# Attention and spectral filter in one kernel: arithmetic of the combination and of the maxima moved to GpSimd, the reciprocal's gate to ScalarE, and a transposition moved one step later

## Chip, cores and metric

One core of one Trainium2 chip. The metric is the device time of one execution in microseconds, as a median over runs; a profiled execution of the same kernel gives the trace, whose span runs from the first to the last instruction.

## What is computed

Two independent parts, joined along the last axis. Part A is an attention with a compressive memory: 2048 rows of width 576, 32 heads of width 18, four segments of 512 rows. In each segment s and head:

```python
logits = qs @ ks.T * scale + causal_mask
a_dot  = softmax(logits) @ vs
pq     = phi(qs)                       # t+1 for t>0, else exp(t)
a_mem  = (pq @ M) / (pq @ z + 1e-6)    # memory of the segments before
o      = g * a_mem + (1 - g) * a_dot   # g = sigmoid(beta), one per head
M, z   = M + phi(ks).T @ vs, z + sum(phi(ks))
```

The heads are joined again and multiplied by wo. Part B is a two-dimensional real FFT of another 2048 x 576 input, a product with a complex filter, and the inverse FFT. All is float32; most matrix products split their inputs into a high and a low part, so that a value x becomes a rounded copy h and a remainder l = x - h, each of which goes through TensorE.

## The kernel before

The order of all instructions on every engine is that in which the Python code issues them; nothing reorders it. Generators that yield let several strands of work be interleaved by hand. The stages are: the forward FFT (to about 78 us), the projections of part A interleaved with the middle of part B (to about 285 us), the inverse FFT with the first ten score blocks of the attention (to about 376 us), and the attention loop with its end (to 818 us). The change lies in the last two.

**The attention loop** (`ATT.attention`, L809 to L877) runs 133 steps t. Four steps, hh = t % 4 = 0 to 3, make one group k = t // 4 of four heads; two groups are one n, eight groups (32 steps) one segment g.

- `s1` (L595 to L616), ten steps ahead: the scores of one head with queries on the partitions, in four matrix products (L602), each followed on VectorE by one reduction with the mask (L606), which puts the row maxima of 128 queries into a column of the tile `mg`. A step has reductions over 128, 384, 512 and 256 elements.
- `mpath` (L617 to L632), once for each group: TensorE transposes the 16 columns of `mg` (L621) into one of the three PSUM buffers that `s1` uses; ScalarE copies the result out as `mf` (L626) and rounds it to bfloat16, `mts[:,0]` (L627); a DMA on GpSimd's queue (L623) writes that as row 108 of the query tile `Qs`; VectorE computes the remainder `mts[:,1]` (L630), and a second DMA writes row 109. These two rows stand against rows of -1 in `Ks` and so subtract the maximum from the scores. The group that is k + 2 in this step starts its `mpath` at hh = 2 and ends it at hh = 3 (L854 to L858). In the prologue (L794 to L808) the first two groups do the same.
- `s2` (L633 to L658): the scores again with keys on the partitions and with the two added rows (L641 to L650), exponentials on ScalarE into P (L642, L647, L651), and after each group four masking operations on GpSimd (L653), 128 x 512 each.
- `pv` (L659 to L670): P times the values (L668), five steps after the exponentials of its group began. `pv_out` copies the result U (L674), and DMAs on SP write it and the sums of the softmax to DRAM (`u_dmas`).

**Background work.** `run_bg(1.2)` (L820 to L826) advances the first generator of the list `bg` 1.2 times in each step; a list `lane` is advanced once in each step, ahead of it. For each segment:

- `recip` (L686 to L706), in `lane`: load the sums as `rx` (SP), three yields, add 1e-6 where asked (L693), reciprocal (L695), multiplication by the gate (L696), rounded copy (L698) and remainder (L699), all on VectorE; store on SP, two yields, load as `rr` or `rd`. It runs seven times: at step 41, 71 and 103 for the memory, at step 45, 77 and 109 and after the loop for the softmax.
- `combine` (L749 to L773), in `bg`: three loads `ux` on SP, two yields, then seven passes t. Pass t spreads the reciprocals over the rows of each head (L765, TensorE into the single PSUM buffer "post"), multiplies `ux` by it (L770, or L768 in segment 0) and adds the memory's part `am` (L771, not in segment 0), both on VectorE. Two passes later the sum is rounded by ScalarE (`oh`, L760) and VectorE computes the remainder (`ol`, L761). Passes 0 and 1 load the fourth and fifth `ux` into buffers that the first two have left.
- `mem1` (L732 to L744): the memory's part of the next segment, with one multiplication on VectorE (L742).
- `oproj` (L774 to L790): the product with wo, 15 matrix products (L786) for each of eight blocks, copied out by ScalarE (L788) from the single "post" buffer, and stored on SP (L789).

After step 132 the rest of `bg` and the last `recip` are advanced in turns (L871 to L875), and then `combine(3)` and `oproj(3)` run alone.

## Time and profile before

| | |
|---|---|
| median of three runs | 826.8 us (824.0 to 826.88) |
| the profiled execution | 820.21 us, span 818.2 us |
| mean granted TensorE clock | 0.96 |
| TensorE, matrix products busy | 727.3 us (89%) |
| VectorE busy | 611.9 us (75%) |
| ScalarE busy | 472.3 us (58%) |
| GpSimd busy | 181.0 us (22%) |

The profiled execution lies 6.6 us under the median of the three runs. Lines of the profile name the line of the kernel, the engine, the operation, the tiles (out<-in) and their shape; in the grouped rows "| busy us, mean ns | idle time before, and what ended it |" follows, in rows in order of time the first two numbers are the start and the duration in us. PE is TensorE, PEld its weight loads, DVE VectorE, ACT ScalarE, POOL GpSimd, SP the queue that issues most DMAs.

### The profile page before, as it was taken

What the parts mean: (1) busy time and instruction counts of PE and PEld (TensorE: products, weight loads), DVE (VectorE), ACT (ScalarE), POOL (GpSimd) and SP (SyncE); (2) the same over time, 40 slices, a digit from 0 to 9 for tenths busy, and PEclk for the clock granted to TensorE, in tenths of its full rate; (3) what the DMA queues carried; (4) which work ended last, traced back from release to release, by engine and by line L of the source; (5) the groups of instructions that cost most, each with busy time, mean ns of one, the idle gap of its engine ahead of it and who ended that gap; (6) DMA issues with size and microseconds to landing.
All of it is one profiled execution on the core that took longest, in us unless ns stands there. A gap on an engine that the chain in (4) does not pass through costs nothing.

```text
span 818.2 us, 14656 instructions
## 1 busy us (share of the span) xinstructions
PE 727.3 (89%) x4751; PEld 489.2 (60%) x4751; DVE 611.9 (75%) x1687; ACT 472.3 (58%) x996; POOL 181.0 (22%) x340
## 2 busy tenths in 40 slices
PE   5998999999999969997988988899988999978856
PEld 4887788797897958895333333335542345523645
DVE  5999877895878779986788888886778767792040
ACT  2665894846846534444777755666555665657111
POOL 2110001001001164441553331331312231323000
PEclk9999999999999989999999989999996999989969
DMA  8883434653534778735576556564463644310221
GB/s 305 264 253 116 158 139 152 223 176 119 196 120 168 255 160 204 223 124 143 146 182 144 123 125 163 132 153 122 115 167 92 156 120 120 115 37 17 61 86 58
DMA packets 82496, 121.27 MB, mean 148 GB/s; under 512 B 9368, under 2 KB 49430, under 8 KB 82284
## 3 DMA queue, kind: packets, MB, share of 16 engines
q1 hardware_dynamic: 74836, 104.29, 44.2%
q0 software_dynamic: 7584, 16.05, 6.7%
q8 instruction: 38, 0.62, 0.3%
q14 instruction: 38, 0.31, 0.1%
HBM read 81.75 MB, written 38.35 MB: 147 GB/s over the span
## 4 chain that ended last, share of the span: by engine, by line
PE 60%; DVE 21%; ACT 8%; issue 6%; DMA 3%; SPq 1%; POOL 0%; DVEq 0%; ACTq 0%
PE pj L440 10%; PE po L786 8%; DVE junk L606 8%; PE s L602 8%; PE pv L668 7%; PE pjv L440 7%; PE i L292 3%; PE i L303 3%; PE s L641 2%; PE s L645 2%; PE pn L735 2%; PE pm L497 1%; DMA Qs<-qkD 1%; PE s L650 1%; DVE eo L123 1%
## 5 line engine op out<-in xcount | busy, mean ns | idle before, releaser
L606 DVE CUSTOM_DVE_ANT_0 junk<-s,mask 128x128 bf16<-128x128 f32 (+3 forms) x512 | 251.3, 491 | 71.6 <-PE s L602 27.1
L602 PE MATMUL s<-Ks,Qs 108*128 108x128 bf16 (+3 forms) x512 | 138.2, 313 | 19.5 <-DVE mg L606 16.2
L602 PEld LDWEIGHTS <-Qs 108*128 108x128 bf16 x512 | 47.1, 100 | 114.4 <-issue 100.9
L668 PE MATMUL pv<-P,vs 128*32 128x512 f32 (+3 forms) x1024 | 100.0, 463 | 1.0 <-issue 0.8
L642 ACT ACTIVATE P<-s 128x512 f32<-128x512 f32 x128 | 76.8, 600 | 41.5 <-PE s L641 34.7
L623 POOL DMA_DIRECT2D Qs<-mts x64 | 31.7, 496 | 247.3 <-ACT mts L627 184.3
L651 ACT ACTIVATE P<-s 128x256 f32<-128x256 f32 x128 | 49.1, 383 | 64.2 <-PE s L650 60.1
L647 ACT ACTIVATE P<-s 128x512 f32<-128x512 f32 x128 | 76.3, 596 | 7.5 <-PE s L646 5.6
L653 POOL TENSOR_SCALAR_AFFINE_SELECT P<-P 128x512 f32<-128x512 f32 x128 | 77.0, 641 | 14.2 <-ACT P L642 13.8
L440 PE MATMUL pj<-xh,wqkh 128*128 128x512 f32 x180 | 71.2, 395 | 0.5 <-ACT Z L151 0.5
L440 PE MATMUL pj<-xh,wqkl 128*128 128x512 f32 x180 | 71.1, 395 | 0.0
L440 PE MATMUL pj<-xl,wqkh 128*128 128x512 f32 x144 | 61.8, 429 | 0.0
L641 PE MATMUL s<-Qs,Ks 110*128 110x512 bf16 x128 | 51.2, 400 | 3.6 <-ACT P L642 2.8
L202 DVE TENSOR_TENSOR Z<-t,t 128x290 f32<-128x290 f32 (+1 forms) x96 | 53.0, 598 | 0.2
L292 PE MATMUL i<-civ,Y 128*128 128x256 f32 (+1 forms) x288 | 44.4, 308 | 9.4 <-DVE T L320 5.3
L202 DVE TENSOR_TENSOR t<-Z 128x580 f32<-128x580 f32 x64 | 48.0, 788 | 0.2
L440 PE MATMUL pjv<-wvh,xh 128*128 128x288 f32 x160 | 48.1, 303 | 0.0
L292 PEld LDWEIGHTS i<-civ,Y 128*128 128x128 f32 (+1 forms) x288 | 39.8, 199 | 11.7 <-DVE T L320 6.3
L440 PE MATMUL pjv<-wvl,xh 128*128 128x288 f32 x160 | 46.2, 295 | 0.0
L645 PE MATMUL s<-Qs,Ks 110*128 110x384 bf16 x128 | 43.5, 340 | 0.1
L606 DVE DVE_READ_ACCUMULATOR2_ANT mg<- 128x1 f32 x512 | 42.4, 83 | 0.1
L788 ACT COPY ob<-po 128x288 f32<-128x288 f32 x32 | 12.7, 398 | 48.3 <-PE po L786 48.1
(140 smaller groups left out, 1518.7 us busy)
## 6 DMA issues: line engine op xcount, KB each, us to landing
qkD<-sp SPq DMA_DIRECT2D x36, 384.0 KB
Qs<-qkD SPq DMA_DIRECT2D x96, 144.0 KB
Ks<-qkD SPq DMA_DIRECT2D x96, 144.0 KB
xin<-xb SPq DMA_DIRECT2D x16, 384.0 KB
cfw<-cfw POOLq DMA_DIRECT2D x16, 384.0 KB, 4.4
civ<-civ POOLq DMA_DIRECT2D x16, 384.0 KB, 7.1
vs<-vD SPq DMA_DIRECT2D x16, 330.0 KB
vD<-vt SPq DMA_DIRECT2D x16, 311.0 KB
```

Of the source, the lines that this page charges most:

```text
L202: v.tensor_tensor(o,a,b,op=op)
L292: nc.tensor.matmul(p[:m,k],Y[i][:,q,c*128:c*128+m],cc[:,hl,o:o+256],start=n==0,stop=n==5)
L440: s.nc.tensor.matmul(out,a,b,start=i==0,stop=i==len(L)-1)
L602: nc.tensor.matmul(out,Q[:108,h,128*i:128*i+128],K[:108,h,:128*(i+1)],start=True,stop=True)
L606: nc.vector.tensor_tensor_reduce(out=junk[:,:w],in0=src,in1=s.mask[:,512-w:],scale=1.0,scalar=-3.0e38, op0=OP.add,op1=OP.max,accum_out=s.m ...
L641: nc.tensor.matmul(p0,kk(0),q(0),start=True,stop=True)
L642: nc.scalar.activation(P[0][:,hh],p0,AF.Exp,scale=SC)
L645: nc.tensor.matmul(p1[:,:384],kk(1),q(128),start=True,stop=True)
L647: nc.scalar.activation(P[1][:,hh],p1,AF.Exp,scale=SC)
L653: sel=lambda x,pat: nc.gpsimd.affine_select(out=x,in_=x,pattern=pat+[[1,128]],compare_op=OP.is_ge,fill=0.0,base=0,channel_multiplier=-1)
L668: nc.tensor.matmul(s.pvt[32*hh:32*hh+32,128*j:],vt[:,j,19*h:19*h+32],mv[0][:,hh,mv[1]],start=jj==0,stop=jj==3,skip_group_check=True)
L786: nc.tensor.matmul(ps,a[t][:r,c],b[:r,t,w],start=i==0,stop=i==14)
```

## The change

Six edits, with line numbers moved by one behind the first added line:

- `mpath`: the remainder `mts[:,1]` is computed on GpSimd instead of VectorE.
- `recip`: a yield is added after the reciprocal; the gate is applied by ScalarE's activation; the rounded copy is ScalarE's; the remainder is GpSimd's.
- `combine`: the remainder `ol` and the addition of `am` go to GpSimd; the multiplications stay on VectorE.
- `attention`: `mpath` starts at hh = 3 instead of 2, with its transposition, copies and first DMA in that step (the DMA now behind the four maskings), and ends at hh = 0 of the next group instead of hh = 3.

```diff
@@ mpath
-        nc.vector.tensor_tensor(mt[:,1],mf,mt[:,0],op=OP.subtract)
+        nc.gpsimd.tensor_tensor(mt[:,1],mf,mt[:,0],op=OP.subtract)
@@ recip
         nc.vector.reciprocal(y,x)
-        nc.vector.tensor_scalar(y,y,gate,None,op0=OP.mult)
+        yield
+        nc.scalar.activation(y,y,AF.Copy,scale=gate)
         w=tp.tile([128,2,128],F32R,name="rw",bufs=1)
-        nc.vector.tensor_copy(w[:,0],y)
-        nc.vector.tensor_tensor(w[:,1],y,w[:,0].bitcast(F32),op=OP.subtract)
+        nc.scalar.copy(w[:,0],y)
+        nc.gpsimd.tensor_tensor(w[:,1],y,w[:,0].bitcast(F32),op=OP.subtract)
@@ combine
-                nc.vector.tensor_tensor(s.ol[u][:r],x[:r],s.oh[u][:r].bitcast(F32),op=OP.subtract)
+                nc.gpsimd.tensor_tensor(s.ol[u][:r],x[:r],s.oh[u][:r].bitcast(F32),op=OP.subtract)
...
-                    nc.vector.tensor_tensor(s.am[t][:r],x[:r],s.am[t][:r],op=OP.add)
+                    nc.gpsimd.tensor_tensor(s.am[t][:r],x[:r],s.am[t][:r],op=OP.add)
@@ attention
-            if hh==3 and m is not None: steps(m,1); m=None
+            if hh==0 and m is not None: steps(m,1); m=None
             steps(a,1)
-            if hh==2 and k+2<32: m=s.mpath(k+2); next(m)
+            if hh==3 and k+2<32: m=s.mpath(k+2); next(m)
             steps(b,1)
-            if hh==2 and m is not None: steps(m,1)
+            if hh==3 and m is not None: steps(m,1)
```

In the changed kernel the gate is L697, the rounded copy L699, the remainder of the reciprocal L700, `oh` L761, `ol` L762, the multiplications L769 and L771, and the addition L772.

## The prediction

> **What bounds the kernel now.** I read the page first, then the table of busy time by stage, then the order of time inside the attention stage.

> ```profile
> span 818.2 us, 14656 instructions
> ...
> PE 60%; DVE 21%; ACT 8%; issue 6%; DMA 3%; SPq 1%; POOL 0%; DVEq 0%; ACTq 0%
> ```

> All edits but two early low parts of maxima act in the attention stage, from 376 us on. On VectorE each step of its loop begins with the 128x128 reduction of L606; between two of these lies a step. Four of them in the table by stage (start:end, length, busy time of PE, PEld, DVE, ACT, POOL, granted clock, DMA share, GB/s): a bare step; the next one, which holds the low part of the maxima (L630); one with one 512-wide operation more on VectorE (L742); and one of a combination, whose three operations stand below it.

> ```profile
> 412.17:414.63 2.46, 1.98 (x16) 0.67 (x11) 1.99 (x8) 1.60 (x6) 1.26 (x1) 1.00 0.91 162
> 414.63:417.09 2.46, 2.21 (x23) 1.05 (x25) 2.14 (x9) 2.42 (x5) 0.75 (x2) 1.00 0.75 150
> 531.89:534.82 2.93, 2.93 (x28) 1.24 (x26) 2.60 (x9) 2.21 (x7) 0.37 (x1) 1.00 0.60 173
> 618.63:622.78 4.15, 3.83 (x15) 1.03 (x15) 3.79 (x12) 2.57 (x5) 1.16 (x2) 0.50 0.46 117
> ```
> ```profile
> 620.86 0.69 DVE L761 TENSOR_TENSOR ol<-am,oh 126x512 fp32r<-126x512 f32 x1
> 621.46 0.68 DVE L770 TENSOR_TENSOR ux<-ux,pb 126x512 f32<-126x512 f32 x1
> 622.17 0.69 DVE L771 TENSOR_TENSOR am<-ux,am 126x512 f32<-126x512 f32 x1
> 622.78 0.28 DVE L606 CUSTOM_DVE_ANT_0 junk<-s,mask 128x128 bf16<-128x128 f32 x1
> ```

> A bare step takes 2.46 us, and the low part of the maxima adds nothing: it fits into a gap between reductions. One operation makes 2.93 us (TensorE is full there), three make 4.15, with the next reduction right behind the third. So VectorE sets the pace of combinations. Whole stretches show what TensorE leaves over:

> ```profile
> 505.99:526.61 20.62, 16.33 (x113) 6.08 (x108) 17.92 (x60) 13.67 (x31) 4.52 (x9) 1.00 0.58 138
> 555.52:604.79 49.27, 47.17 (x368) 29.12 (x366) 35.36 (x133) 29.16 (x67) 13.36 (x24) 0.97 0.48 125
> 604.79:630.92 26.13, 20.07 (x113) 6.96 (x114) 21.54 (x64) 13.39 (x31) 4.51 (x8) 0.80 0.53 137
> 663.93:712.25 48.32, 45.86 (x371) 28.32 (x373) 35.43 (x133) 29.57 (x67) 13.30 (x24) 1.00 0.44 113
> 714.72:729.95 15.23, 10.64 (x61) 3.51 (x55) 14.27 (x36) 7.00 (x15) 3.37 (x6) 0.78 0.17 45
> 479.13:483.41 4.28, 3.29 (x25) 0.93 (x20) 3.81 (x13) 2.14 (x4) 0.19 (x1) 1.00 0.14 39
> 491.74:495.75 4.01, 3.65 (x28) 1.19 (x26) 3.58 (x12) 2.92 (x6) 0.00 (x0) 1.00 0.44 109
> ```

> Rows 1, 3 and 5 are the combinations of segments 0, 1 and 2 (the third without its end): VectorE nearly full, TensorE idle for 4.3, 6.1 and 4.6 us. Rows 2 and 4 are projection stretches, where TensorE is the bound (2.1 and 2.5 us idle). Rows 6 and 7 are the first two steps with a reciprocal.

> **The change part by part.** The rows of the grouped instructions that leave VectorE with the reciprocal:

> ```profile
> L698 DVE CAST rw<-ry 128x128 fp32r<-128x128 f32 x7 | 1.6, 227 | 0.2
> L699 DVE TENSOR_TENSOR rw<-ry,rw 128x128 fp32r<-128x128 f32 x7 | 2.0, 293 | 0.2
> L696 DVE TENSOR_SCALAR ry<-ry,g 128x128 f32<-128x128 f32 x4 | 1.1, 286 | 0.1
> ```

> *Combinations in the loop.* In segment 1 a multiplication also waited for its load; the row of that stretch:

> ```profile
> L770 DVE TENSOR_TENSOR ux<-ux,pb 126x512 f32<-126x512 f32 (+1 forms) x5 | 3.4, 681 | 2.2 <-PE s L602 2.2
> ```

> Five multiplications (0.68 us each) remain on VectorE. Segment 0: six steps, 20.62 us, become five of 2.93 and one of 2.46, 17.1: 3.5 saved. Segment 1: 26.13 become 17.1 plus that wait of 2.2 us (kept), 19.3: 6.8, but TensorE was idle for 6.1 only, which I take. Segment 2: three steps, 15.23 us, become 2.46, one with two multiplications (2.93 + 0.7 = 3.6) and 2.93; a multiplication pushed into the next step costs 0.5: 5.7, capped at 4.6. Sum 14.2 us. What is late next is TensorE, which is full in the 2.93 us step.

> *Gate, cast and low part of the reciprocal.* 0.29 + 0.23 + 0.29 = 0.81 us leave VectorE in each of seven places. In rows 6 and 7 TensorE's idle time allows 0.8 and 0.4: 1.2. In the two projection stretches the gate also met the masking on GpSimd:

> ```profile
> 574.05 1.23 POOL L653 TENSOR_SCALAR_AFFINE_SELECT P<-P 128x512 f32<-128x512 f32 x2
> 574.80 1.73 DVE L696 TENSOR_SCALAR ry<-ry,gt 128x128 f32<-128x128 f32 x1
> ```

> The gate took 1.73 us instead of 0.29. Per stretch 1.73 + 0.23 + 0.29 + 0.81 = 3.1 us go, of which TensorE's idle time lets through at most 2.1 and 2.5. I take 1.8 each: 3.6. Gain so far 19.0.

> [...] A reduction has one input in SBUF, the mask, and GpSimd's L575 ran beside reductions in 1397 to 1419 ns without a long case (row below). [...]

> *GpSimd's new load.* It has not run these operations; the nearest rows (L575 with its shortest, median and longest case):

> ```profile
> L575 POOL TENSOR_TENSOR wol<-ob,woh x5: 1397/1406/1419, 392.9 to 419.7; 126x576 fp32r<-126x576 f32 x5
> ```
> ```profile
> L277 POOL TENSOR_TENSOR Y<-Z,Y 128x512 fp32r<-128x512 f32 x16 | 19.9, 1243 | 34.6 <-ACT Y L276 34.6
> L512 POOL TENSOR_TENSOR Mst<-mm,Mst 126x126 f32<-126x126 f32 x8 | 3.4, 428 | 20.1 <-DVE mm L505 20.1
> L623 POOL DMA_DIRECT2D Qs<-mts x64 | 31.7, 496 | 247.3 <-ACT mts L627 184.3 <-DVE mts L630 54.0 <-ACT oh L760 3.3
> L653 POOL TENSOR_SCALAR_AFFINE_SELECT P<-P 128x512 f32<-128x512 f32 x128 | 77.0, 641 | 14.2 <-ACT P L642 13.8
> DMA to landing us min/median/max: 1.5/2.7/5.4
> ```

> I take 1.24 us per addition or low part (same shape), 0.43 for small ones. Segment 1 or 2 needs 10 x 1.24 + 8 maskings x 0.6 + 4 issues x 0.5 + 2 x 0.43 = 20.1 us of GpSimd within about eight steps of 2.6 us, 21: it nearly fills them. Call s the start of the masking ahead of the first addition. It takes 4 x 0.6, an issue 0.5; the next masking stands behind eight moved operations, a small one and an issue, so it can start at s + 2.9 + 8 x 1.24 + 0.9 = s + 13.7. Its data come four steps of some 2.9 us after s, at s + 11.6: 2 us late. Queued behind GpSimd:
> - The matrix product that reads the mask comes two steps later: nothing is lost.
> - ScalarE's copy oh waits for GpSimd's addition, exponentials behind it: up to 0.6 us each.
> - Loads of ux 3 and 4 wait on SP for additions 0 and 1, some 2 us later than now, with SP's other loads behind them; then multiplication 3 waits for the load, reductions behind it: 0 to 2.
> - The rows of maxima go out behind the masking: the second at s + 13.7 + 2.4 + 0.5 + 1.24 + 0.43 = s + 18.3. It is read nine steps after s, less 2 us by which TensorE leads, at s + 22: 3.7 us remain, and a landing takes 2.7, at most 5.4 (from 595 us on): 0 to 2.

> From 0 to 8 us for both segments; I take 2, since the median landing is in time. The yield itself moves a combination one or two steps later; the background work stays the same, and as many copies of projections are left behind the loop's last step as before (16), so I cost it at nothing but for the end.

> *Transposition one step later.* In the worst row TensorE waited there for VectorE's last maxima:

> ```profile
> 611.56 0.28 PE L621 MATMUL mt<-ident,mg 128*16 128x128 f32 x1 [2.87 <-DVE mg L606]
> ```

> Its data are then a step old and the wait goes. In bare steps VectorE is the bound, so nothing is gained; in combinations it is part of the idle time above. The low part costs nothing where it was, and 0.43 us on a GpSimd that is idle outside the combinations (the two early ones stand behind L277, two 1.24 us at most, with five steps to go); the PSUM buffer is held as long as before.

> *The end.* Here VectorE is free, and both moves lengthen the path.

> ```profile
> 770.86 0.40 ACT L788 COPY ob<-po 128x288 f32<-128x288 f32 x1 [2.38 <-PE po L786]
> ```
> ```profile
> 771.60 0.95 DVE L695 RECIPROCAL ry<-rx 128x128 f32<-128x128 f32 x1 [16.34 <-DMA rx<-rD]
> ```
> ```profile
> 783.40 0.69 DVE L771 TENSOR_TENSOR am<-ux,am 126x512 f32<-126x512 f32 x1
> ```
> ```profile
> 791.47 0.62 ACT L760 CAST oh<-am 72x512 fp32r<-72x512 f32 x1 [1.30 <-DVE am L771]
> ```
> ```profile
> L517 ACT ACTIVATE nid<-ident 128x128 bf16<-128x128 f32 x1 | 0.3, 313 | 0.0
> ```

> The added yield puts gate and cast (0.31 us each by L517) on ScalarE's queue just ahead of the copy that started at 770.86. They wait for the reciprocal until 772.55, so the copy starts at 773.2. With one PSUM buffer the next projection waits for it: 2.3 us. In combination 3 the last addition is the eighth operation of GpSimd's queue: 783.4 + 8 x 1.24 = 793.3, handovers 0.3, copy 0.62: oh is ready at 794.3 instead of 792.1, and the low parts keep ahead of TensorE: 2.3 us. Together 4.6 (2.3 if one of them is hidden, 6 with slower handovers).

> [...]

> **Sum.** 14.2 + 1.2 + 3.6 - 2 - 4.6 = 12.4 us. The profiled execution took 820.21 us, so it would take 807.8. The three timed runs lie higher (median 826.8, 824.0 to 826.88); the same step from their median gives **814.4 us**.

> **Rivals.**
> 1. GpSimd takes over as the bound in combinations 1 and 2: all the queueing above at its upper end costs 8 us instead of 2, giving 820.4. For it: 20.1 of 21 us. Against: half of these waits fall on work that is ahead.
> 2. TensorE bounds the combination steps already, so their 14.2 us don't come: 826.8 - 4.8 + 6.6 = 828.6. For it: clock 0.80 and 0.78 in rows 3 and 5. Against: the 2.87 us wait, and VectorE without a gap at the end of the 4.15 us step.
> 3. Slower: GpSimd's two-input operations lengthen beside reductions, to twice 1.24 us. The 20 in segments 1 and 2 add 24.8 us: 839.2. It decides from 12.4 / 20 = 0.6 us more each, an operation of 1.86 us. For it: 0.29 became 1.73 when VectorE met GpSimd. Against: at most 1.42 us for 576 elements beside reductions.

> **How the numbers follow.** Forecast 0.62 (own range 807 to 820), rival 1 0.20, rival 2 0.09, rival 3 0.09. The best case is TensorE's whole idle time without queueing, 15.0 + 1.2 + 4.6 = 20.8, less 2.3 at the end: 808.3, and 2 less for the scatter of the runs, 806. The range goes from there to rival 2 at 829 and leaves out rival 3 and part of the tails. Half a per cent, 4.1 us, is about what a measurement can tell from no change: below 822.7 is faster. Forecast with most of rival 1 gives 0.74; 0.15 the same (the rest of it and rival 2); 0.11 slower (rival 3, a little of rival 2).

> **What would show it.** Right: one multiplication per combination step and steps near 2.9 us; L762 and L772 on POOL near 1240 ns; L697 at the end waiting for the reciprocal, the projection behind it 2.3 us late; the stretch from the last loads of ux to the next projection 2 us longer. Wrong: moved operations far above 1.3 us; waits of L641 for Qs or of the pv product for masking; VectorE waiting for ux; gaps of TensorE unchanged in the combinations.

## The result, and the profile after

The changed kernel took 817.9 us (median of ten runs, 812.4 to 824.9) where the kernel before took 826.8 in the same series (821.9 to 831.8): ratio 0.9886, 95% interval 0.9845 to 0.9927, so 9.4 us less by the ratio. The ratio leaves out the slowest of the ten runs (824.9 us), which counts as slow, so it gives 9.4 us and not the 8.9 between the medians. Forecast were 814.4, range 806 to 829. The profiled execution took 812.37 us, 7.8 less than that of before; the step forecast was 12.4. The trace of after is the fastest of its ten runs, and that of before lies below all ten of its own.

The page of after, span and chain:

```profile
span 810.6 us, 14493 instructions
...
PE 61%; DVE 15%; ACT 8%; DMA 6%; issue 4%; POOL 3%; SPq 1%; DVEq 0%; ACTq 0%; POOLq 0%
```

VectorE's share of the chain fell from 21% to 15%; loads and GpSimd came in. Where the 7.6 us of span went is read from the table by stage (start:end, length, busy time of PE, PEld, DVE, ACT, POOL, granted clock, DMA share, GB/s). First before, in rows that the prediction didn't show: to step 50, the two whole projection stretches, the loop's last step and what follows it, up to the last loads of ux, up to the first copy of the last projection, and its other seven blocks.

```profile
376.39:505.99 129.60, 112.23 (x790) 43.82 (x794) 105.36 (x422) 88.88 (x193) 48.10 (x78) 0.93 0.60 148
526.61:604.79 78.18, 74.03 (x545) 39.08 (x541) 58.43 (x221) 48.19 (x108) 22.43 (x40) 0.98 0.52 133
630.92:714.72 83.80, 79.15 (x579) 40.52 (x581) 62.70 (x239) 52.43 (x116) 23.12 (x41) 0.98 0.48 125
729.95:764.15 34.20, 30.86 (x222) 13.22 (x218) 10.94 (x20) 20.77 (x46) 8.16 (x14) 1.00 0.08 20
764.15:779.99 15.84, 12.82 (x84) 11.24 (x83) 1.76 (x4) 2.97 (x7) 0.00 (x0) 1.00 0.26 79
779.99:795.07 15.08, 7.33 (x20) 4.62 (x19) 9.72 (x15) 3.09 (x5) 0.00 (x0) 0.55 0.30 98
795.07:818.20 23.13, 15.88 (x105) 14.23 (x105) 0.00 (x0) 3.18 (x8) 0.00 (x0) 1.00 0.14 52
```

The same of after, with the three combinations (rows 2, 4 and 6) in their places:

```profile
376.16:502.35 126.19, 107.84 (x790) 42.93 (x794) 101.67 (x405) 89.98 (x198) 55.00 (x92) 0.97 0.63 148
502.35:521.36 19.01, 15.43 (x102) 5.65 (x97) 14.70 (x53) 11.42 (x26) 9.37 (x13) 0.91 0.69 165
521.36:598.38 77.02, 73.62 (x551) 38.47 (x550) 54.46 (x208) 50.83 (x115) 28.17 (x51) 1.00 0.52 134
598.38:616.34 17.96, 15.53 (x114) 5.97 (x112) 14.74 (x54) 12.04 (x27) 11.43 (x14) 1.00 0.74 185
616.34:702.01 85.67, 81.86 (x583) 40.99 (x576) 58.64 (x225) 54.57 (x124) 32.22 (x55) 0.94 0.45 120
702.01:711.59 9.58, 7.91 (x59) 3.15 (x61) 7.79 (x27) 6.15 (x14) 6.54 (x10) 1.00 0.32 103
711.59:744.81 33.22, 30.85 (x219) 12.51 (x211) 6.71 (x16) 21.71 (x49) 18.20 (x23) 1.00 0.10 24
744.81:764.55 19.74, 15.30 (x92) 13.71 (x91) 0.95 (x1) 3.68 (x9) 0.45 (x1) 0.91 0.24 78
764.55:782.52 17.97, 7.87 (x20) 4.72 (x19) 3.43 (x5) 3.09 (x5) 12.35 (x10) 0.60 0.26 82
782.52:810.60 28.08, 20.77 (x105) 18.89 (x105) 0.00 (x0) 3.19 (x8) 0.00 (x0) 0.74 0.11 43
```

| stage | before | after | difference | forecast |
|---|---|---|---|---|
| to step 50 | 129.60 | 126.19 | -3.4 | -1.2 |
| combination, segment 0 | 20.62 | 19.01 | -1.6 | -3.5 |
| projection stretch 1 | 78.18 | 77.02 | -1.2 | -1.8 |
| combination, segment 1 | 26.13 | 17.96 | -8.2 | -6.1 |
| projection stretch 2 | 83.80 | 85.67 | +1.9 | -1.8 |
| combination, segment 2 | 15.23 | 9.58 | -5.7 | -4.6 |
| GpSimd's queue | | | in the rows above | +2 |
| last step and behind it | 34.20 | 33.22 | -1.0 | 0 |
| to the last loads of ux | 15.84 | 19.74 | +3.9 | +2.3 |
| to the first copy of the last projection | 15.08 | 17.97 | +2.9 | +2.3 |
| seven more blocks | 23.13 | 28.08 | +5.0 | 0 |

With 0.2 us by which the loop starts earlier the differences add up to the span's 7.6. Up to the last step the loop gained 18.1 us, 17.0 were forecast; behind it the end lost 10.8, not 4.6. The clock column tells what the largest loss is: in the last seven blocks it was 1.00 before and 0.74 after.

### The profile page after: what moved, and what is told of

Its sections match the earlier page's. It is cut to its first block, busy times and chain, and to the rows that moved or that the text cites. A ratio compares the mean times of both kernels' runs of the same rounds, so it can differ in the third digit from the quotient of the medians.

```text
span 810.6 us, 14493 instructions
## 1 busy us (share of the span) xinstructions
PE 724.3 (89%) x4751; PEld 492.3 (61%) x4751; DVE 571.7 (71%) x1599; ACT 475.5 (59%) x1010; POOL 241.6 (30%) x414
## 4 chain that ended last, share of the span: by engine, by line
PE 61%; DVE 15%; ACT 8%; DMA 6%; issue 4%; POOL 3%; SPq 1%; DVEq 0%; ACTq 0%; POOLq 0%
PE pj L440 10%; PE po L787 9%; PE pv L668 8%; PE s L602 8%; PE pjv L440 7%; DVE junk L606 7%; PE i L303 3%; PE i L292 3%; PE s L641 2%; PE s L645 2%; PE pm L497 1%; PE pn L736 1%; DMA civ<-civ 1%; PE s L650 1%; DMA ux<-uD 1%
## 5 line engine op out<-in xcount | busy, mean ns | idle before, releaser
L606 DVE CUSTOM_DVE_ANT_0 junk<-s,mask 128x128 bf16<-128x128 f32 (+3 forms) x512 | 251.1, 490 | 81.5 <-PE s L602 31.5
L602 PE MATMUL s<-Ks,Qs 108*128 108x128 bf16 (+3 forms) x512 | 136.0, 309 | 15.6 <-DVE mg L606 13.8
L653 POOL TENSOR_SCALAR_AFFINE_SELECT P<-P 128x512 f32<-128x512 f32 x128 | 77.5, 635 | 135.8 <-ACT P L642 132.1
L602 PEld LDWEIGHTS <-Qs 108*128 108x128 bf16 x512 | 46.1, 99 | 104.9 <-issue 91.4
L668 PE MATMUL pv<-P,vs 128*32 128x512 f32 (+3 forms) x1024 | 97.2, 452 | 0.8 <-POOL P L653 0.4
L642 ACT ACTIVATE P<-s 128x512 f32<-128x512 f32 x128 | 76.7, 599 | 33.6 <-PE s L641 26.3
L641 PE MATMUL s<-Qs,Ks 110*128 110x512 bf16 x128 | 50.1, 392 | 3.3 <-ACT P L642 1.8
L292 PE MATMUL i<-civ,Y 128*128 128x256 f32 (+1 forms) x288 | 42.6, 300 | 8.8 <-DMA civ<-civ 3.5
L487 POOL MEMSET vt<- 128x32 f32 x16 | 2.3, 161 | 151.7 <-PE pm L497 85.3
L292 PEld LDWEIGHTS i<-civ,Y 128*128 128x128 f32 (+1 forms) x288 | 38.1, 190 | 12.0 <-DVE T L325 3.7
L787 PE MATMUL po<-woh,oh 126*128 126x288 f32 (+1 forms) x160 | 33.4, 341 | 12.7 <-ACT ob L789 9.0
```

The lines of the kernel that those rows point to most:

```text
L292: nc.tensor.matmul(p[:m,k],Y[i][:,q,c*128:c*128+m],cc[:,hl,o:o+256],start=n==0,stop=n==5)
L602: nc.tensor.matmul(out,Q[:108,h,128*i:128*i+128],K[:108,h,:128*(i+1)],start=True,stop=True)
L606: nc.vector.tensor_tensor_reduce(out=junk[:,:w],in0=src,in1=s.mask[:,512-w:],scale=1.0,scalar=-3.0e38, op0=OP.add,op1=OP.max,accum_out=s.m ...
L641: nc.tensor.matmul(p0,kk(0),q(0),start=True,stop=True)
L642: nc.scalar.activation(P[0][:,hh],p0,AF.Exp,scale=SC)
L653: sel=lambda x,pat: nc.gpsimd.affine_select(out=x,in_=x,pattern=pat+[[1,128]],compare_op=OP.is_ge,fill=0.0,base=0,channel_multiplier=-1)
```

## The experiments

**The theory** was: the gain is VectorE's relief in the combinations; the end takes part of it back, by the gate in ScalarE's queue, by combination 3's longer chain, and by TensorE's clock (0.74 instead of 1.00 in the last seven blocks), taken to fall when TensorE idles longer. **Rival A**: the later transposition brings the gain. **Rival B**: the low clock at the end is an accident of one trace. Times are medians of 6 to 12 runs. A ratio is against the kernel before on the same chip, and 0.001 of it is 0.8 us.

### 1. The parts alone

*Only the combination's edits, on the kernel before:*

```diff
-nc.vector.tensor_tensor(s.ol[u][:r],x[:r],s.oh[u][:r].bitcast(F32),op=OP.subtract)
+nc.gpsimd.tensor_tensor(s.ol[u][:r],x[:r],s.oh[u][:r].bitcast(F32),op=OP.subtract)
...
-nc.vector.tensor_tensor(s.am[t][:r],x[:r],s.am[t][:r],op=OP.add)
+nc.gpsimd.tensor_tensor(s.am[t][:r],x[:r],s.am[t][:r],op=OP.add)
```

> The kernel before with only the combination's additions and low parts on GpSimd. Between the two traces the three combinations in the loop became 1.6, 8.2 and 5.65 us shorter, the stretch from the last reciprocal loads' products to the first copy of the last projection 2.9 us longer, and the last seven projection blocks 4.95 us longer. Theory (VectorE relieved in the combinations brings the gain, the end takes part of it back): the loop gains 12 to 15 us, the end loses 5 to 8, so 5 to 9 us less than before (ratio 0.989 to 0.994). Rival A (the later transposition, which ends TensorE's waits of 2 to 3 us for the last maxima, brings the gain): the combinations keep those waits and gain at most 4 us, the end loses as much, so 1 to 4 us more than before. Rival B (the slow last blocks are a clock accident of one trace, not tied to the end's changed order): the end loses only 2 to 3, so 9 to 12 us less than before.

819.05 us, ratio 0.9922 (0.9888 to 0.9956): 6.4 us less, as the theory had it. Its table by stage, the combinations of segments 0 and 1:

```profile
508.05:525.61 17.56, 15.21 (x104) 5.85 (x100) 15.04 (x56) 12.52 (x29) 9.11 (x12) 1.00 0.64 157
603.68:626.98 23.30, 20.22 (x101) 6.66 (x102) 15.15 (x55) 12.37 (x29) 13.63 (x16) 0.71 0.62 154
```

Segment 0 comes out as forecast (17.1). Segment 1 has VectorE busy for 15 us instead of 21.5 but is at clock 0.71, and saves 2.8, not 8.2: its first multiplication began after 2.72 us of idle VectorE, TensorE waited 2.69 us for the maxima that it held up, and 13.65 us at half clock followed.

*Only the transposition's place, on the kernel before:* `mpath` starts at hh = 3 and ends at hh = 0; its low part stays on VectorE.

> The kernel before with only the start and end of the transposition of the maxima moved one step later; the low part stays on VectorE. Theory: nothing, within 1.5 us of before, since VectorE is the bound in bare steps and in combinations and its work is unchanged. Rival A: the waits of TensorE for the last maxima (2.87 us in the worst row of before) go and with them most of the gain, 6 us or more less than before.

822.75 us, 0.9969 (0.9935 to 1.0003): 2.6 us less, with an interval that reaches no change. Rival A's 6 us or more lie outside it.

*Only the reciprocal's edits, on the kernel before:*

```diff
-        nc.vector.tensor_scalar(y,y,gate,None,op0=OP.mult)
+        yield
+        nc.scalar.activation(y,y,AF.Copy,scale=gate)
...
-        nc.vector.tensor_copy(w[:,0],y)
-        nc.vector.tensor_tensor(w[:,1],y,w[:,0].bitcast(F32),op=OP.subtract)
+        nc.scalar.copy(w[:,0],y)
+        nc.gpsimd.tensor_tensor(w[:,1],y,w[:,0].bitcast(F32),op=OP.subtract)
```

> The kernel before with only the reciprocal's edits (one yield more, gate and rounded copy on ScalarE, low part on GpSimd). Theory: 2 to 4 us less in the loop (steps 41 and 45 were 0.6 and 0.9 us shorter in the trace of after), 3 to 4 us more behind it, where the copy of a projection block stands behind the gate on ScalarE's queue: between 1 us less and 2 us more than before. The prediction had 4.8 us less in the loop and 2.3 more at the end, so 2.5 us less.

827.12 us, 1.0027 (1.0000 to 1.0054): 2.2 us more. Alone it is no gain; the prediction had 2.5 us less for it. The order of time shows a wait that nobody had forecast, at the first multiplication of the first combination:

```profile
510.45 0.69 DVE L769 TENSOR_TENSOR am<-ux,pb 126x512 f32<-126x512 f32 x1 [4.01 <-DMA ux<-uD]
```

The bracket is VectorE's idle time ahead of it, and what ended it: the load of ux. Before, this multiplication did not wait. In the changed kernel the same wait is 1.39 us, and TensorE's next transposition waits behind it:

```profile
506.06 0.69 DVE L769 TENSOR_TENSOR am<-ux,pb 126x512 f32<-126x512 f32 x1 [1.39 <-DMA ux<-uD]
507.61 0.28 PE L621 MATMUL mt<-ident,mg 128*16 128x128 f32 x1 [2.25 <-DVE mg L606]
```

The three parts add up to -6.8 us, the whole is -9.4; with their intervals that is no difference.

### 2. The end undone

*Both ends:* in the changed kernel, the last reciprocal has its gate, copy and low part on VectorE without the yield, and the last combination its additions and low parts.

```diff
+        if dst is s.rrD[3]:
+            nc.vector.tensor_scalar(y,y,gate,None,op0=OP.mult)
...
-nc.gpsimd.tensor_tensor(s.am[t][:r],x[:r],s.am[t][:r],op=OP.add)
+(nc.vector if g==3 else nc.gpsimd).tensor_tensor(s.am[t][:r],x[:r],s.am[t][:r],op=OP.add)
```

> The changed kernel, with the last reciprocal's gate, copy and low part back on VectorE without the added yield, and the additions and low parts of the last combination back on VectorE; the loop keeps the change. Theory: the end of before comes back, so of the 11.8 us that the end lost between the two traces (3.9 at the reciprocal, 2.9 at the combination, 5.0 in the last blocks) 7 to 12 us come back: 806 to 811 us, ratio to before 0.974 to 0.981. Rival B (the 5.0 us of the last blocks are a clock accident): 4 to 7 us come back, 811 to 814, and TensorE's clock in the last blocks is low in some runs of either kernel.

808.46 us, 0.9807 (0.9760 to 0.9855): 15.9 us less than before, 6.5 less than the changed kernel by the ratios, whose intervals barely overlap. Taken as measured, the loop alone is worth 16 us, and the changed end takes 6.5 of them. The time lies in the theory's range, but the 6.5 us lie in rival B's 4 to 7, so this run does not decide between the two.

*Only the last combination undone* (the second half of that diff):

> The changed kernel with the additions and low parts of the last combination alone back on VectorE; the last reciprocal stays as changed. Theory: the combination's chain gives back the 2.9 us by which it was longer in after, and with less idle time of TensorE in it one or two of the three slow blocks become fast, 1.7 us each: 812 to 814, and the rest of what the version with both ends undone gained (it came to 808.5) belongs to the reciprocal. Rival: if the last combination costs nothing of its own, the time of after, 816 to 819, and the reciprocal has it all.

814.1 us, 0.9863 (0.9829 to 0.9896), between the two: by the ratios 1.9 us for the combination and 4.6 for the reciprocal. The intervals overlap, so the sum is shown and the split is not.

*TensorE kept busy in the changed end:* 32 extra products in the last combination and in the first block, their result read by nothing.

```diff
+    def warm(s,n):
+        p=s.ps.tile([128,512],F32,name="warm",tag="s2")
+        for _ in range(n): s.nc.tensor.matmul(p,s.woh[:,0,:128],s.woh[:,1,:512],start=True,stop=True)
...
+                if g==3: s.warm((9,3,3,3,4)[t])
...
+                    if g==3 and tb==0 and hf==0 and i in (3,4): s.warm(5)
```

> The changed kernel, in which TensorE gets extra matrix products in the last combination and ahead of the first low-part products of the last projection, 32 in all, into a PSUM tile that nothing reads; they fill its waits for the loads and for GpSimd and add work but no dependence. In the trace of after TensorE idled from 765.0 to 768 and had gaps to 780; its granted clock was 0.50 from 768 to 795, and three blocks of the last projection took 4.46, 4.50 and 4.26 us where the later four took 2.78. Theory (the idle time ahead of them sets the low clock): with the waits filled the clock stays at 1 and the blocks take 2.8, so 4 to 6 us less than after, 812 to 814 (ratio to before 0.982 to 0.985). Rival B (the low clock is an accident of that trace): the time of after, 816 to 819.

812.39 us, 0.9835 (0.9801 to 0.9870): 4.2 us less than the changed kernel by the ratios, though it does more. The last seven blocks, in the table by stage:

```profile
784.35:804.55 20.20, 15.89 (x105) 14.23 (x105) 0.00 (x0) 3.19 (x8) 0.00 (x0) 1.00 0.12 45
```

Clock 1.00, every block 2.8 us. The intervals of the two ratios overlap, but the mean clock of the runs says the same as the trace: 0.966 to 0.973 in five of the six (0.954 in the sixth, 822.91 us), 0.944 to 0.963 in the ten of the changed kernel. So filling TensorE's idle time raised the clock of the changed end: 1.00 in these seven blocks, 0.74 without the extra products.

Rival B falls only in part. Among the last seven blocks the traces of before and of the transposition alone have no slow one (4.3 us and more), that with both ends undone has one (4.35 us), and two versions of part 4, with the same undone end, have two each (4.46 and 4.50 us). Three come in the trace of after alone. So the same end gets none to two, and the 5.0 us of the table are not all the change's.

*The same on the version with both ends undone* (9, 3, 3, 3 and 2 extra products in the combination, none in the projection):

> The changed kernel with the last reciprocal and the last combination back as before, and 20 extra matrix products in the last combination into a PSUM tile that nothing reads, to fill TensorE's waits. Without them this version took 808.5 us, with its clock at 0.50 from 768.8 to 785.4 and one slow block of 4.35 us. Theory: the clock stays at 1, the slow block (1.6) and the first block's products at half speed (1.9 us for five instead of 0.93, 15 in all, about 1.5 us) go: 805 to 807. Rival (the low clock of the end isn't tied to idle time): 808 to 809.

808.82 us, 0.9812 (0.9771 to 0.9853): nothing gained, against the theory. Three stretches of 3.41 us in the combination, each as long as one window of the clock's grid (see the last section), and what followed:

```profile
766.96:770.37 3.41, 1.93 (x10) 1.24 (x8) 0.73 (x2) 0.00 (x0) 0.00 (x0) 1.00 0.91 303
770.37:773.78 3.41, 2.87 (x9) 1.49 (x9) 3.34 (x6) 1.24 (x2) 0.00 (x0) 1.00 0.34 92
773.78:777.19 3.41, 2.30 (x7) 0.92 (x6) 3.38 (x6) 1.24 (x2) 0.00 (x0) 1.00 0.09 32
777.19:790.85 13.66, 12.22 (x45) 10.88 (x45) 2.18 (x4) 1.42 (x3) 0.00 (x0) 0.50 0.06 22
```

TensorE was busy for 57%, 84% and 67% of these stretches. Behind the third the clock went from 1.00 to 0.50, just as the projection began; behind the first, less busy, it stayed at 1.00. So the extra products had only put the fall off (without them the clock was at 0.50 from 768.8 us on), and in these stretches the busy share alone does not tell when it comes. The clock then stayed at 0.50 for 13.66 us, through two blocks, before each of which TensorE waited 0.49 to 0.53 us for ScalarE's copy out of the single PSUM buffer.

### 3. A second PSUM buffer for the last projection

```diff
-ps=s.ps.tile([128,288],F32,name="po",tag="post")
+ps=s.ps.tile([128,288],F32,name="po",tag="s2" if g==3 and hf else "post")
```

*With the extra products:*

> The same as the version with the end of before and the extra products, and the last projection's blocks take turns in two PSUM buffers, so that a block doesn't wait for ScalarE's copy of the one ahead. These waits were 0.49 to 0.53 us before each of the last seven blocks. Theory: 7 x 0.47 = 3.3 us less than without the second buffer, 802 to 804. Rival (the products' weights or operands are the limit there): the same 805 to 807.

798.12 us, 0.9692 (0.9649 to 0.9735): 9.9 us less than without the buffer, three times the expected 3.3; the intervals do not touch.

*Without them:*

> The version with both ends undone (808.5 us), with the last projection's blocks in two PSUM buffers in turns and no extra products. With the extra products the second buffer brought 10.7 us (808.8 to 798.1), where 3.3 were expected from the waits alone. Theory: the waits of 0.45 us between blocks also kept the granted clock at 0.50 (it came back only in stretches of 3.4 us without a gap), so without the extra products the second buffer brings the 3.3 us and the slow blocks: 801 to 804. Rival (the extra products and the buffer are needed together): 804 to 806 at best.

803.75 us on a chip where before took 827.46, 0.9697 (0.9651 to 0.9744): the same ratio as with them, within the intervals. The buffer does it alone. Its last seven blocks, in the fastest of the six runs:

```profile
777.44:792.14 14.70, 13.91 (x105) 13.67 (x103) 0.00 (x0) 3.20 (x8) 0.00 (x0) 1.00 0.16 61
```

From copy to copy a block takes 2.0 us (the row ends with the last copy), where it was 2.77: the whole turn of handover, copy and handover went, not only the 0.45 us that the profile counts as idle. And the clock rose within the first block (0.50 up to 777 us, 0.96 in the microsecond behind it, 1.00 from there on). That it rose because nothing interrupts TensorE any more fits and wasn't tried by itself. Together the seven blocks took 13.94 us from the first copy to the last, against 21.04 in the version with both ends undone.

*In addition, two buffers for the projection of segment 2* (`g>=2` in the diff, with the extra products):

> The version that took 798.1 us (both ends undone, extra products in the last combination, the last projection's blocks in two PSUM buffers in turns), with two buffers in turns for the projection of segment 2 as well, whose eight blocks also run mostly behind the loop, 2.77 us each with 0.45 to 0.5 us of waiting. Theory: up to 7 x 0.45 = 3 us less, 795 to 797, if the last reciprocal's chain of transfers doesn't become the bound. Rival (that chain ends last: the reciprocal waited 15 us for its load in after, and the last combination waits for it): the same 797 to 799.

797.51 us, 0.9652 (0.9607 to 0.9696). This is the fastest version, 3.5% below the kernel before; its step of 3.3 us to the version with g==3 is within the intervals, and its time lies in the rival's range. Whether the buffer helps there too is open.

### 4. Who sets the pace in the combinations

*Additions on VectorE again in all segments,* low parts on GpSimd, from the version with both ends undone:

> The version with both ends undone (808.5 us), with the additions of the combinations on VectorE everywhere; the low parts stay on GpSimd. Theory (VectorE sets the pace of the combinations): the five additions of 0.69 us in each of segments 1 and 2 come back, of which some 0.5 us each count, since TensorE left 0.5 us in such a step: 5 us more, 812 to 815. Rival 1 of the prediction (GpSimd is the bound in the combinations): GpSimd has 12.5 us less to do there, so not slower, 803 to 809.

815.88 us, 0.9864 (0.9821 to 0.9908): 4.7 us more than that version, a little above the theory's range, and with intervals that overlap. Segment 1 of this kernel:

```profile
601.78:625.05 23.27, 20.28 (x114) 6.90 (x112) 19.83 (x58) 12.50 (x27) 8.44 (x11) 0.75 0.63 163
```

and of the version with both ends undone:

```profile
601.77:620.60 18.83, 16.09 (x115) 6.14 (x113) 14.72 (x54) 12.56 (x27) 12.29 (x14) 1.00 0.73 180
```

GpSimd does 3.9 us less, VectorE 5.1 more, and the stretch is 4.4 us longer. Part of that is the clock (0.75 against 1.00). But the step with the first addition still ran at 1.00, and it is 1.3 us longer (this kernel, then the version with both ends undone):

```profile
606.72:610.86 4.14, 3.65 (x29) 1.46 (x24) 3.29 (x11) 2.84 (x9) 3.68 (x7) 1.00 0.73 207
606.70:609.54 2.84, 2.35 (x22) 1.03 (x21) 2.51 (x9) 1.79 (x6) 2.68 (x5) 1.00 0.79 216
```

VectorE is the bound, not GpSimd: rival 1 falls. Three of the five additions also took 1.04 to 1.43 us instead of 0.69, each while GpSimd ran a low part: in this half of the move the operations of both engines were longer where they met (the second of the two low parts below took 1.71 us, a later one 1.26). One of them, and what GpSimd did:

```profile
617.71 1.17 DVE L777 TENSOR_TENSOR am<-ux,am 126x512 f32<-126x512 f32 x1
617.06 2.95 POOL L767 TENSOR_TENSOR ol<-am,oh 126x512 fp32r<-126x512 f32 x2 [6.09 <-ACT oh L766]
```

*The transposition at its old place,* from the same version:

> The version with both ends undone (808.5 us; ratio to before 0.981), with the transposition of the maxima back at its old place and its low part still on GpSimd. Alone, the later transposition gave a ratio of 0.997 with an interval from 0.9935 to 1.0003. Theory (it brings nothing of its own): 806 to 811. Rival C (once VectorE is relieved, TensorE's wait for the last maxima is what is late next in the combinations, so the move is needed there): one wait of 2 to 3 us in most combination groups and some in the projection stretches, 4 us or more above 808.5, 812.5 to 817.

813.92 us, 0.9837 (0.9794 to 0.9879): 2.5 us more by the ratios, inside both intervals. The median lies in rival C's range; on this chip before took 827.46 us, and by the ratio the step is less than rival C's 4. The two traces have the same span (806.5 and 806.3 us), but this one is the fastest of six runs, of which four took 813.5 us or more. Segment 1 has the same length in both:

```profile
601.51:620.23 18.72, 15.74 (x107) 6.00 (x106) 14.66 (x53) 12.04 (x28) 11.43 (x14) 1.00 0.73 193
```

Its transpositions' grouped row, and one bare step with the transposition at its new place (order of time, after):

```profile
L621 PE MATMUL mt<-ident,mg 128*16 128x128 f32 x32 | 9.0, 280 | 1.8 <-DVE mg L606 1.4
```
```profile
414.90 0.28 PE L621 MATMUL mt<-ident,mg 128*16 128x128 f32 x1 [0.46 <-DVE mg L606]
```

At the old place hardly any wait is left once VectorE is relieved; the 2.87 us of before were VectorE's lateness, not the place's fault. At the new place the transposition waits 0.46 us in most bare steps, although its data are a step older. Rival C falls for the combinations, as far as the trace goes; a gain of the move of up to some 2.5 us is neither shown nor excluded.

## Why the prediction held, and where it missed

**The loop: right.** Forecast 19.0 less 2 of queueing; the version with both ends undone measured 15.9, the trace up to the last step 18.1. VectorE was the bound in the combinations, and TensorE's whole idle time of segments 1 and 2 came back, and more: 8.2 and 5.7 instead of 6.1 and 4.6. The cap by idle time was too low because the rows it was taken from had clocks of 0.80 and 0.78: with the idle time went the low clock (1.00 and 1.00 in after), so the products got shorter too. Rival 2 had read these clocks as a sign that TensorE was the bound; they went with its waiting.

How far single traces can be trusted here: six other versions above run the loop code of the changed kernel (both ends undone, only the last combination undone, two with extra products, and two with the second buffer at `g==3`). In these seven traces segment 1 took 17.9 to 21.3 us (before 26.1) and segment 2 9.6 to 11.0 (before 15.2); with the additions back it was 23.3 and 11.7. So the gain of these two does not hang on one trace.

**Segment 0: wrong.** 1.6 us in this trace, not 3.5, and over the seven traces none is shown: 18.7 to 21.9 us, before 20.6. The step "five of 2.93 and one of 2.46" gave a wait to segment 1 and none to segment 0. With the combination's edits alone it holds (17.56 us); with the reciprocal's edits the loop reaches the multiplication sooner after the load's issue than the load lands, 1.39 us in after and 4.01 alone. The load of ux is late next; the prediction had named VectorE waiting for ux as a sign of being wrong. Behind this wait the seven traces spend 3.4 to 10.2 us of the combination at half clock, and their lengths follow these. In segment 1 the wait of 2.2 us that the prediction kept did not come back in after. That it had been a wait for the load was an inference: its row names the product L602.

**Reciprocals: not shown as told.** To step 50 the gain was 3.4 instead of 1.2, but in after that stretch also has 10 us less at half clock than in before. In the first projection stretch it was 1.2 instead of 1.8. Alone, the reciprocal's edits saved 2.8 us up to step 50 and lost 5.6 in the combination of segment 0, at the load above. The second stretch lost 1.9. This is no cost of the edits: of the seven traces, three have at most 0.5 us at half clock there and took 81.1 us, the other four have 10 to 11 us and took 85.5 to 85.8. The same three steps (95 to 97) of two of them are

```profile
639.01:653.43 14.42, 12.94 (x60) 3.68 (x59) 7.18 (x27) 6.09 (x14) 3.77 (x7) 0.64 0.49 134
```

in after and

```profile
643.27:653.14 9.87, 8.38 (x60) 2.86 (x59) 7.10 (x26) 5.77 (x14) 3.77 (x7) 1.00 0.49 136
```

with both ends undone: 4.5 us by the clock alone, on the same work. The wait of TensorE in them is the same too (order of time, after and both ends undone):

```profile
641.98 1.98 PE L736 MATMUL pn<-pq,Mst 72*72 72x512 f32 x2 [1.20 <-DVE am L743]
646.25 1.08 PE L741 MATMUL pn<-pq,Mst 72*72 72x512 f32 x2 [1.20 <-DVE am L748]
```

**GpSimd's price: right,** 1.24 and 0.43 us assumed:

```profile
L762 POOL TENSOR_TENSOR ol<-am,oh 126x512 fp32r<-126x512 f32 (+1 forms) x20 | 25.4, 1276 | 5.6 <-ACT oh L761 5.4
L772 POOL TENSOR_TENSOR am<-ux,am 126x512 f32<-126x512 f32 (+1 forms) x15 | 19.0, 1270 | 15.0 <-DVE ux L771 15.0
L630 POOL TENSOR_TENSOR mts<-mf,mts 16x128 bf16<-16x128 f32 x32 | 13.4, 420 | 0.4
```

No operation was lengthened by the reductions (the 35 long ones took 1.25 to 1.30 us), so rival 3 falls. What made the 1.73 us of the gate beside the masking in before, no run shows. The 2 us of queueing aren't seen in the combinations, although GpSimd was nearly full, as forecast: from its first addition in segment 1 on (606.30 to 622.00 us of after) it was busy for 14.24 of 15.70 us.

**The transposition: right for a wrong reason.** It changed next to nothing, but "the wait goes" failed: 0.46 us in most bare steps are new. They cost nothing: four bare steps take 9.85 us in after (4 x 2.46), as long as before. The product of the transposition goes into one of the three PSUM buffers that the reductions empty; that it waits for the buffer fits the rows and wasn't tried by itself.

**The end: the mis-sized step.** Both mechanisms are in the trace as told, and near the forecast size. The reciprocal (order of time):

```profile
752.27 0.95 DVE L695 RECIPROCAL ry<-rx 128x128 f32<-128x128 f32 x1 [15.03 <-DMA rx<-rD]
753.26 0.40 ACT L697 ACTIVATE ry<-ry,g 128x128 f32<-128x128 f32 x1 [3.07 <-DVE ry L695]
753.69 0.30 ACT L699 CAST rw<-ry 128x128 fp32r<-128x128 f32 x1
754.03 0.40 ACT L789 COPY ob<-po 128x288 f32<-128x288 f32 x1
754.48 1.57 PE L787 MATMUL po<-woh,oh 126*128 126x288 f32 x5 [2.00 <-ACT ob L789]
```

The copy stood behind gate and cast, and TensorE's wait grew from 0.49 to 2.00 us; but then its five products took 1.57 us instead of 0.93. The copy came 1.5 us late, and the block behind it took 1.5 us more at half clock. And combination 3's last part:

```profile
777.48 1.25 POOL L772 TENSOR_TENSOR am<-ux,am 72x512 f32<-72x512 f32 x1
778.77 0.62 ACT L761 CAST oh<-am 72x512 fp32r<-72x512 f32 x1 [1.82 <-POOL am L772]
779.44 0.61 PE L787 MATMUL po<-woh,oh 72*128 72x288 f32 x1 [1.83 <-ACT oh L761]
```

From the start of the first multiplication to the end of the last `oh` it took 11.61 us, before 9.41: 2.2 us more. So the terms of 2.3 us each came as 1.5 and 2.2. What the sum lacked is a third, the clock behind them, which it put at nothing. Behind the wait of 2.00 us at the reciprocal the clock was 0.50 for one stretch of 3.42 us, and in the last combination, where it was 0.50 in before too, it stayed so for longer. The table by stage of after, cut where the clock changes:

```profile
754.36:757.78 3.42, 3.30 (x14) 3.30 (x15) 0.00 (x0) 0.07 (x1) 0.17 (x1) 0.50 0.14 41
757.78:768.02 10.24, 5.45 (x34) 4.42 (x33) 0.24 (x1) 1.20 (x3) 0.00 (x0) 1.00 0.39 133
768.02:795.32 27.30, 19.06 (x63) 15.35 (x64) 3.20 (x5) 4.28 (x8) 12.35 (x10) 0.50 0.10 31
795.32:807.60 12.28, 9.45 (x63) 8.26 (x61) 0.00 (x0) 2.00 (x5) 0.00 (x0) 1.00 0.13 49
```

27.30 us on end at half clock, where the trace of before has 13.7 (781.0 to 794.7). Three projection blocks fell into them, and each took 1.5 to 1.7 us more. The runs put the end at 6.5 us instead of 4.6 (0.9886 less 0.9807); filling TensorE's waits brought 4.2 back. With 1.1 us less in the loop this is the difference between 12.4 forecast and 9.4 measured. These steps of a few us between versions are within or at the edge of their intervals. And since an undone end got up to two slow blocks, how much of the third term is the change's stays open.

So the forecast came near by terms that partly cancelled: segment 0 and the end brought less than forecast, and segments 1 and 2 more.

## What to carry to other kernels

Here moving elementwise work from a full VectorE to GpSimd paid where VectorE set the pace (8.2 and 5.7 us in the combinations of segments 1 and 2), even at nearly twice the time per operation (1.27 us against 0.69), and cost where that work was on a lone chain (2.2 us in the last combination): so make such a move by stage, not by function. Count a new wait of TensorE as idle time, and reckon with a second loss by the clock that may follow it (behind a wait of 1.20 us 4.5 us more, or nothing); and where products alternate with copies out of a single PSUM buffer, give them a second one before anything cleverer (it brought 9 us here, the whole change 9.4).

## What the runs showed of the hardware

In these two traces half speed was easier to fall into than to leave, and no single threshold of the busy share lies between the two. At full speed, in the windows of 3.41 us of this grid from 300 us on, every one with TensorE busy for 51% or less was followed by half speed and none with 65% or more; between these both happened (in before 1.76 us busy of the 3.41 from 606.93 us on were followed by 1.00, and 1.88 us of those from 627.41 us on by 0.50). In the trace of part 2 above the clock stayed behind 57% and fell behind 67%. At half speed no window with less than 90% was followed by a rise: the clock was 0.50 through three blocks of 4.0 us of products with 0.49 to 0.53 us between them (after, 782.98 to 795.3 us). With the second PSUM buffer the seven blocks had no such waits and ran at 1.00; it was the largest gain of all single steps tried on the end (9.9 us with the extra products). Even a full window was not always enough for a rise. In the version with only the combination's edits TensorE was busy throughout these two, and the clock rose one window later:

```profile
612.73:616.14 3.41, 3.41 (x18) 1.28 (x17) 2.56 (x10) 1.95 (x4) 2.80 (x4) 0.50 0.65 172
616.14:619.56 3.42, 3.42 (x17) 1.04 (x16) 1.87 (x9) 2.09 (x5) 3.42 (x5) 0.50 0.63 131
```

The same wait of TensorE (1.20 us) was followed by 4.5 us more at 0.64 in one trace of the same loop and by nothing in another, which ran on at 1.00. The ten runs of the changed kernel line up with their mean clock, from 812.4 us at 0.963 to 824.9 at 0.944. That the place of the grid is what differs between them fits and isn't shown, since only one of them was traced.
